# A second SiLU matmul by one level of Strassen's algorithm, with the weight parts of the first one's stage spread between its products

## The chip, the cores and the metric

The kernel runs on one core of one Trainium2 chip. The metric is device microseconds from the start of the program to its end, as the median of three runs. The core's engines run their own instruction streams: TensorE (PE) multiplies, ScalarE (ACT), VectorE (DVE) and GpSimd (POOL) work on tiles element by element, and SyncE (SP) issues the DMA transfers. They wait for one another at semaphores.

## The reference

Pooled attention, then two feed-forward layers on 4608 tokens of width 512; every array is fp32:

```python
def _moe2_ref(x, w_in, w_out):          # x: 4608 x 512
    h = x @ w_in                        # w_in: 512 x 2048
    g = h * (1.0 / (1.0 + np.exp(-h)))  # SiLU
    return (g @ w_out)                  # w_out: 2048 x 512

def reference(**kwargs):
    attn_out = _attn_ref(q, k, v)       # 8 x 8 x 576 x 64, keys and values pooled by 8
    x = ...                             # 4608 x 512
    x = _moe_ref(x, ...)                # SoLU and layer norm, 512 -> 1024 -> 512
    return _moe2_ref(x, ...)
```

The change touches `_moe2_ref` alone.

## The kernel before, in words

An fp32 value is kept as two parts of type fp32r, hi and lo: hi is a copy made by ACT (`AF.Copy`), lo is the difference, made by DVE or POOL (`sub`). One fp32 product is three matmuls: hi with hi, hi with lo, lo with hi.

The program has three stages. The first computes attention and the SoLU layer and puts `x` into DRAM (`x2d`); it also turns the weights of the last two matmuls into fp32 and keeps them in DRAM (`w2if`, `w2of`). The change leaves it alone but for the shape of `w2of`.

The second stage is the first SiLU matmul, already done by one level of Strassen's algorithm (in Winograd's form: seven products and fifteen additions for eight products). It has 12 steps `n`: half the columns of `w_in` (`half`) by six groups `g` of 768 tokens. A step has four pairs `i`, and `hidden2(n, i, hooks)` computes one: seven products of six matmuls of 128x384, each into a PSUM bank, and the additions that combine them. DVE makes `u2`, `u3`, `gt[0,0]` (c11), `gt[0,1]` (c12) and `gt[1,0]` (c21) out of PSUM (L654), ACT copies `m1` and `m5`, POOL adds two. PE may be eight products ahead, since there are eight banks. Between these operations the four `hooks` stand, in which the parts for later products are made:

- `tokens(n + 1)`: sums and differences of the next step's token blocks (T1 to T4 on POOL), their hi copies on ACT, their lo parts on DVE (`lo`, L517, 128x768). They are given out over the four pairs. Raw tokens come by `load_tokens`, 1.5 MB into `x2r`, which has one buffer.
- `quad(q)`: the weight parts of a quarter of `w_in`, six functions, from `w2r` (one buffer, `load_quad`, 1 MB). `quad(1)` is made ahead of the stage; `quad(2)` between the pairs (5,2), (5,3) and (6,0), and `quad(3)` after (6,0) and (6,1).
- in n=11, where no tokens are left, the hi and lo parts of the first seven blocks of `w_out` (`split_w2o`, lo on POOL).

When a pair is over, ACT applies SiLU and SP stores the 768 KB of `gt` to `gd` in DRAM (`finish_pair`, called in the next pair).

The third stage is the second SiLU matmul. `project2(c, f)` multiplies block `f` (of 16) of chunk `c` (of 9, 512 tokens each) by `w_out`: four PSUM banks, three matmuls of 128x512 each, 1728 matmuls in all (L722). Two steps ahead of it, `split_g` makes hi (ACT, L117) and lo (DVE, L118) of g, which `load_g` reads back from `gd` in loads of four blocks. The other nine blocks of `w_out` are split beside the first steps. `store2` copies the four banks (two by ACT, two by DVE) and stores 256 KB each.

PE follows program order throughout. From the second stage on ACT, DVE, POOL and SP follow it too (`manual_schedule`), so an instruction that waits holds up everything behind it on its engine.

Of the kernel before, what the change touches and what calls it, by code (L numbers as in the profile page):

```python
# [89 lines left out]
):  # L90
    nc = tc.nc
    const = ctx.enter_context(tc.tile_pool(name="const", bufs=1, side="left"))
    stage = ctx.enter_context(tc.tile_pool(name="stage", bufs=2, side="left"))
# [582 lines left out]
    w2oh, w2ol = {}, {}
    graw, g_t, o_t = {}, {}, {}

    w2s = {}

    def load_w2o(f):
        w2s[f] = stage.tile([P, DM], F32, tag="w", name="w2s", bufs=3)
        nc.sync.dma_start(w2s[f], w2of[f])

    def split_w2o(f):
        if f < 7:
            t = pools["te"].tile([P, 2, DM], F32R, tag=f"t{f}", name="w2o")
        else:
            t = pools["w2o"].tile([P, 2, DM], F32R, tag=f"w2o{f}", name="w2o")
        w2oh[f], w2ol[f] = t[:, 0], t[:, 1]  # L690
        nc.scalar.activation(w2oh[f], w2s[f], AF.Copy)
        sub(nc.gpsimd, w2ol[f], w2s[f], w2oh[f].bitcast(F32))

    def load_g(c, b):
        if (c, b) == (0, 0):
            raw = pools["x2r"].tile([P, 4, GO], F32, tag="x2r", name="gr")
        else:
            raw = pools["gr"].tile([P, 4, GO], F32, tag=f"gr{b % 3}", name="gr")
# [8 lines left out]
    def split_g(c, f):
        gh = pools["gs"].tile([P, GO], F32R, tag=f"gh{f % 4}", name="gh")
        gl = pools["gs"].tile([P, GO], F32R, tag=f"gl{f % 4}", name="gl")
        split(gh, gl, graw[c, f // 4][:, f % 4])  # L710
# [2 lines left out]
    def project2(c, f):
        gh, gl = g_t.pop((c, f))
        if f == 0:
            o_t[c] = [bank("op") for t in range(4)]
        for t in range(4):
            ts = slice(t * P, (t + 1) * P)
            for m, (l, r) in enumerate(
                ((gh[:, ts], w2oh[f]), (gh[:, ts], w2ol[f]), (gl[:, ts], w2oh[f]))  # L720
            ):
                nc.tensor.matmul(  # L722
                    o_t[c][t], l, r, start=(f == 0 and m == 0), stop=(f == FC2 - 1 and m == 2)
                )

    def store2(c):
        for t in range(4):
            ob = pools["out"].tile([P, DM], F32, tag=f"ob{t}", name="ob")
            if t % 2:
                nc.vector.tensor_copy(ob, o_t[c][t])  # L730
            else:
                nc.scalar.activation(ob, o_t[c][t], AF.Copy)
            r0 = c * GO + t * P
            nc.sync.dma_start(out[r0 : r0 + P], ob)
# [154 lines left out]
    load_tokens(1)
    for f in quad(1):  # L890
        f()
    N2 = NSUB * NG2
    for n in range(N2):
        work = tokens(n + 1) if n + 1 < N2 else [[] for _ in range(4)]
        if n == 0:
            work = [[], work[0], work[1], [lambda a=a, b=b: (a(), b()) for a, b in zip(work[2], work[3])]]
        for i in range(NPAIR):
            if (n, i) == (0, 0):
                continue
            if (n, i) in ((NG2 - 1, 0), (NG2, 0)):  # L900
                load_quad(2 + (n == NG2))
            hooks = work[i]
            if n == N2 - 1:
                for f in range(2 * i, min(2 * i + 2, 7)):
                    load_w2o(f)
                    hooks = hooks + [lambda f=f: split_w2o(f)]
            hidden2(n, i, hooks)
            if (n, i) in ((NG2 - 1, 2), (NG2, 0)):
                q2 = quad(2 + (n == NG2))
                for f in q2[:3]:  # L910
                    f()
# [10 lines left out]
    open_pool("gr", 1, "right")
    open_pool("w2o", 1, "right")
    open_pool("out", 1, "right")
    steps = [(c, f) for c in range(NGO) for f in range(FC2)]
    LAG = 2
    load_g(0, 1)
    for i in range(len(steps) + LAG):
        if i < len(steps):
            c, f = steps[i]  # L930
            if i < 9:
                load_w2o(i + 7)
            if f % 4 == 0 and i + 8 < len(steps):
                load_g(steps[i + 8][0], steps[i + 8][1] // 4)
            split_g(c, f)
            if i < 9:
                split_w2o(i + 7)
        if i >= LAG:
            c, f = steps[i - LAG]
            project2(c, f)  # L940
            if f == FC2 - 1:
                store2(c)


# [38 lines left out]
```

## Time and profile before

| | us |
|---|---|
| median of three runs (1421.16, 1422.57, 1426.73) | 1422.57 |
| the profiled execution | 1423.88 |
| its span in the trace | 1422.1 |
| PE busy (7416 matmuls) | 1321.4, 93% |
| DVE busy | 787.4, 55% |
| ACT busy | 647.5, 46% |
| POOL busy | 537.6, 38% |

The second stage lies at 614 to 1016 of the span, the third from there to the end. A busy share is a mean over stages that differ; which engine the end waits for is to be read stage by stage from the chain, from the idle times in front of PE's instructions, and from the timeline. Matmuls overlap, so what one costs is the distance from one to the next and not its own duration.

### The profile page before, as it was taken

The numbers are of one execution on the slowest core, as the hardware profiler recorded it, in microseconds if no ns is written. First come the engines' busy times: TensorE is split into PE (matmuls) and PEld (weight loads), VectorE is DVE, ScalarE is ACT, GpSimd is POOL, SyncE is SP. The second block draws the span as 40 slices with busy tenths as digits, with TensorE's granted clock in tenths as the row PEclk, the third lists the DMA queues.
The fourth block names the chain that finished last, engine by engine and source line by source line (L and its number), as shares of the span: only waits on it lengthen the run. The fifth ranks groups of instructions, "written<-read, shape, count | busy, mean of one in ns | idle before, by whom it ended". The sixth has DMA issues, their size and how long they took to land.

```text
span 1422.1 us, 20311 instructions
## 1 busy us (share of the span) xinstructions
PE 1321.4 (93%) x7416; PEld 1192.7 (84%) x7416; DVE 787.4 (55%) x1161; ACT 647.5 (46%) x1624; POOL 537.6 (38%) x737
## 2 busy tenths in 40 slices
PE   2689999999999998999899979999899999999998
PEld 2478789988989897998899969999788888888887
DVE  6896566757756556247677676766343222222222
ACT  4784656555555555344444544445432222222221
POOL 5674443535444335226556656656430000000000
PEclk9799999999999999999999999999899999999999
DMA  6655154534433201033434543444733444214440
GB/s 223 209 171 163 59 156 134 156 119 133 147 104 112 89 31 60 30 119 122 160 134 155 186 141 133 156 158 172 240 111 104 148 148 148 90 61 146 148 148 30
DMA packets 85651, 186.91 MB, mean 131 GB/s; under 512 B 6192, under 2 KB 27696, under 8 KB 83504
## 3 DMA queue, kind: packets, MB, share of 16 engines
q1 hardware_dynamic: 85552, 185.63, 39.0%
q8 instruction: 58, 0.95, 0.3%
q14 instruction: 41, 0.34, 0.1%
HBM read 120.59 MB, written 65.01 MB: 131 GB/s over the span
## 4 chain that ended last, share of the span: by engine, by line
PE 55%; DVE 6%; DMA 3%; ACT 3%; issue 3%; POOL 1%; SPq 0%; DVEq 0%; ACTq 0%; POOLq 0%
PE op L722 27%; PE m L644 15%; PE xp L498 6%; PE hp L428 5%; DVE t L517 2%; DMA x2r<-x2d 2%; DVE gt L654 1%; PE tp L478 1%; DVE u L654 1%; DVE wt L517 1%; PE sp L299 1%; ACT w2s L538 1%; ACT gt L626 1%; PE av L403 0%; DVE w2s L517 0%
## 5 line engine op out<-in xcount | busy, mean ns | idle before, releaser
L644 PE MATMUL m<-t,w2s 128*128 128x384 f32 x2016 | 362.8, 340 | 23.5 <-DVE gt L654 8.0
L644 PEld LDWEIGHTS m<-t,w2s 128*128 128x128 f32 x2016 | 355.7, 191 | 30.2 <-DVE gt L654 11.3
L722 PE MATMUL op<-w2o,gh 128*128 128x512 f32 x1152 | 357.2, 392 | 6.6 <-ACT gh L117 6.6
L722 PEld LDWEIGHTS op<-w2o,gh 128*128 128x128 f32 x1152 | 217.8, 189 | 52.5 <-ACT gh L117 7.4
L118 DVE TENSOR_TENSOR gl<-gr,gh 128x512 fp32r<-128x512 f32 x144 | 106.4, 751 | 263.4 <-ACT gh L117 263.4
L722 PE MATMUL op<-w2o,gl 128*128 128x512 f32 x576 | 225.4, 391 | 0.2 <-DVE gl L118 0.2
L117 ACT ACTIVATE gh<-gr 128x512 fp32r<-128x512 f32 x144 | 89.0, 629 | 258.8 <-PE op L722 208.3
L498 PE MATMUL xp<-lnh,w1oh 128*128 128x256 f32 x576 | 168.1, 292 | 0.6 <-ACT lnh L117 0.3
L498 PE MATMUL xp<-lnl,w1oh 128*128 128x256 f32 x576 | 164.3, 285 | 1.2 <-DVE lnl L118 1.2
L498 PE MATMUL xp<-lnh,w1ol 128*128 128x256 f32 x576 | 164.1, 285 | 0.0
L654 POOL TENSOR_TENSOR gt<-u,m 128x384 f32<-128x384 f32 x96 | 120.1, 1271 | 115.4 <-DVE u L654 76.6
L722 PEld LDWEIGHTS op<-w2o,gl 128*128 128x128 f32 x576 | 108.7, 189 | 23.7 <-DVE gl L118 1.1
L428 PE MATMUL hp<-w1ih,xTh 128*128 128x512 f32 x288 | 119.8, 416 | 7.9 <-DVE e L447 7.8
L428 PE MATMUL hp<-w1il,xTh 128*128 128x512 f32 x288 | 115.9, 402 | 0.6 <-POOL w1il L150 0.6
L428 PE MATMUL hp<-w1ih,xTl 128*128 128x512 f32 x288 | 115.9, 402 | 0.0
L317 ACT ACTIVATE pr<-sp,st 128x72 f32<-128x72 f32 x288 | 88.3, 331 | 59.0 <-POOL st L309 58.8
L498 PEld LDWEIGHTS xp<-lnl,w1oh 128*128 128x128 f32 x576 | 111.7, 194 | 1.5 <-DVE lnl L118 1.4
L498 PEld LDWEIGHTS xp<-lnh,w1oh 128*128 128x128 f32 x576 | 111.5, 194 | 1.7 <-DVE lnl L118 1.1
L498 PEld LDWEIGHTS xp<-lnh,w1ol 128*128 128x128 f32 x576 | 111.7, 194 | 0.0
L672 ACT ACTIVATE gt<-gt 128x768 f32<-128x768 f32 x48 | 40.7, 847 | 148.6 <-DVE gt L654 148.6
L517 DVE TENSOR_TENSOR t<-x2r,t 128x768 fp32r<-128x768 f32 x36 | 60.4, 1679 | 25.5 <-ACT t L582 25.5
L428 PEld LDWEIGHTS hp<-w1ih,xTh 128*128 128x128 f32 x288 | 56.3, 195 | 20.4 <-issue 7.6
(109 smaller groups left out, 2098.9 us busy)
## 6 DMA issues: line engine op xcount, KB each, us to landing
gd<-gt SPq DMA_DIRECT2D x48, 768.0 KB, 4.2
gr<-gd SPq DMA_DIRECT2D x24, 1024.0 KB, 6.8
x2r<-x2d SPq DMA_DIRECT2D x12, 1536.0 KB, 8.1
gr<-gd SPq DMA_DIRECT2D x24, 512.0 KB, 6.2
q<-qT SPq DMA_DIRECT2D x36, 256.0 KB, 3.1
raw<-kT SPq DMA_DIRECT2D x32, 288.0 KB, 3.4
x2d<-xo SPq DMA_DIRECT2D x18, 512.0 KB, 3.4
out<-ob SPq DMA_DIRECT2D x36, 256.0 KB, 3.0
```

The lines of the kernel that those rows point to most:

```text
L117: nc.scalar.activation(hi, src, AF.Copy)
L118: nc.vector.tensor_tensor(lo, src, hi.bitcast(F32), op=ALU.subtract)
L299: nc.tensor.matmul(sp[done : done + n, p // 2, (p % 2) * 2 * SP : (p % 2 + 1) * 2 * SP], q[:, p, done : done + n], kbd[b % 2][:, p, :], st ...
L317: behind["ACT"] = nc.scalar.activation(pr[:, g, h], sv[:, g, h], AF.Exp, scale=SCALE, bias=st[:, 0, g, h : h + 1], accum_out=st[:, 1, g, h ...
L428: nc.tensor.matmul(hp[:, f], l, r, start=(n == 1 and m == 0), stop=(n == KC and m == 2))
L478: nc.tensor.transpose(tp[:, k * P : (k + 1) * P], e[:, f, k * P : (k + 1) * P], ident)
L498: nc.tensor.matmul(xp[:, :GW], l, r, start=(k == 0 and m == 0), stop=(k == FC1 - 1 and m == 2))
L517: eng.tensor_tensor(dst, a, b, op=ALU.subtract)
L644: nc.tensor.matmul(to, wt[:, a, o : o + P], tk[:, b, k], start=(k == 0 and m == 0), stop=(k == 1 and m == 2),)
L654: eng.tensor_tensor(dst, a, b, op=ALU.add)
L672: nc.scalar.activation(gt[:, 0], gt[:, 0], AF.Silu)
L722: nc.tensor.matmul(o_t[c][t], l, r, start=(f == 0 and m == 0), stop=(f == FC2 - 1 and m == 2))
```

## The change

The third stage gets Strassen's form too. A chunk of 512 tokens is two halves of 256, an output block is 256 columns, and the 16 blocks of f are four sets (`NSET`) of two blocks each from the upper and lower half of `w_out`. A product is 12 matmuls of 128x256: seven a set, 252 products in all, 3024 matmuls. A bank holds a product summed over the four sets of a chunk, so seven banks are in use.

- `sums_g(q)` makes S1 and S2 of a set's g on POOL (two 128x512 operations). `prepare(n)` makes the parts of product `n`: a copy by ACT, a difference by DVE, and before S3A and after A12 one more DVE operation. They go into a ring of nine (`NRING`), and `prepare(n + 9)` stands behind product `n`.
- `w2o_unit(fs, ...)` makes the weight parts for one or two f in seven functions: seven ACT copies, seven DVE subtractions, four POOL subtractions. For f = 0, 1 it runs in pair (11,0), for f = 2 in (11,1); `sums_g(0)` and `prepare` 0 to 6 in (11,2) and (11,3). f = 3 is made between products 0 to 6, f = 4, 5 between 7 to 13, f = 6, 7 between 14 to 20.
- `combine(c, j)` stands behind each product of a chunk's last set: five DVE adds out of PSUM, two ACT copies and two POOL adds a chunk, and two stores of 512 KB.
- In the second stage `quad(1)` goes into the hooks of (0,1), the tokens of n=1 into (0,2) and (0,3); in n=5 the tokens of n=6 into the first two pairs and `quad(2)` into the last two; in n=6 `quad(3)` into the first two and the tokens into the last two. `spread` deals the functions out over a pair's four hooks. `load_quad` makes two loads, for quad 2 behind (1,0), for quad 3 behind (5,3); `load_tokens(1)` stands ahead of `load_quad(1)`.
- At the hand-over, the pools of the second stage are closed, and `load_g(1)`, `load_g(2)` and the late weights stand on SP behind the last pair's store.

```diff
+NSET = FC2 // 4
+NRING = 9
...
     def load_quad(q):
-        w2r[q] = pools["wr"].tile([P, 4, 512], F32, tag="w2r", name="w2r")
-        nc.sync.dma_start(w2r[q], w2if[q])
+        w2r[q] = [pools["wr"].tile([P, 2, 512], F32, tag=f"w2r{h}", name="w2r") for h in range(2)]
+        for h in range(2):
+            nc.sync.dma_start(w2r[q][h], w2if[q][:, 2 * h : 2 * h + 2])
...
+    def w2o_unit(fs, load, to, temps):
...
+        def tmp(k, a, b):
+            t[k] = temps(k).rearrange("p (f d) -> p f d", d=256)[:, :n]
+            sub(nc.gpsimd, t[k], a, b)
+        def put(j, src):
+            w = to(j)
+            nc.scalar.activation(w[:, :, 0], src, AF.Copy)
+            sub(nc.vector, w[:, :, 1], src, w[:, :, 0].bitcast(F32))
...
+        def first():
+            tmp(1, b12, b11)
+            tmp(2, b22, t[1])
+            put(0, b11)
...
+    def sums_g(q, temps):
...
+        nc.gpsimd.tensor_tensor(s1, a21, a22, op=ALU.add)
+        sub(nc.gpsimd, s2, s1, a11)
...
+    def prepare(n):
...
+        if j == S3A:
+            sub(nc.vector, a21, a11, a21)
...
+        nc.scalar.activation(ring[n][:, 0], src, AF.Copy)
+        sub(nc.vector, ring[n][:, 1], src, ring[n][:, 0].bitcast(F32))
+        if j == A12:
+            sub(nc.vector, a12, a12, s2)
...
+    def product2(n):
...
+        for i in range(2):
+            w = wo[2 * s + i, j]
+            for h in range(2):
+                ts = slice(h * P, (h + 1) * P)
+                for m, (l, r) in enumerate(((0, 0), (0, 1), (1, 0))):
+                    nc.tensor.matmul(
+                        op[:, 256 * h : 256 * h + 256], t[:, l, i, ts], w[:, r],
...
+    load_tokens(1)
     load_quad(1)
-    load_tokens(1)
-    for f in quad(1):
-        f()
...
         if n == 0:
-            work = [[], work[0], work[1], [lambda a=a, b=b: (a(), b()) for a, b in zip(work[2], work[3])]]
+            work = [[], quad(1), work[0] + work[1], work[2] + work[3]]
+        elif n == NG2 - 1:
+            q2 = quad(2)
+            work = [work[0] + work[1], work[2] + work[3], q2[:3], q2[3:]]
+        elif n == NG2:
+            q3 = quad(3)
+            work = [[lambda: None] + q3[:3], q3[3:], work[0] + work[1], work[2] + work[3]]
+        elif n == N2 - 1:
...
+            g0 = [lambda: sums_g(0, wt_tmp)] + [lambda m=m: prepare(m) for m in range(7)]
+            work = [u0, u1, g0[:4], g0[4:]]
...
+            hidden2(n, i, spread(work[i]))
+            if n == 1 and i == 0:
+                load_quad(2)
+            if (n, i) == (NG2 - 1, NPAIR - 1):
+                load_quad(3)
...
+    load_g(1)
+    load_g(2)
...
+    late = late_w2o([3])
+    sums_g(1, s_tmp)
+    nxt = late_w2o([4, 5])
+    prepare(7)
+    prepare(8)
+    for n in range(NM):
...
+        product2(n)
+        if s == NSET - 1:
+            combine(c, j)
+        if q <= 2:
+            late[j]()
+        m = n + NRING
+        if m < NM:
...
+            prepare(m)
```

What stands in a row on DVE in pair (5,0), before. `u`, `m` and `gt` are the pair's additions, `t` the lo parts of the next step's tokens:

```order
L654 TENSOR_TENSOR u_8415<-m,m_8413 128x384
L654 TENSOR_TENSOR u_8416<-m,u_8415 128x384
L517 TENSOR_TENSOR t_8444<-x2r,t_8444 128x768
L654 TENSOR_TENSOR gt<-m,m_8413 128x384
L517 TENSOR_TENSOR t_8456<-x2r,t_8456 128x768
L654 TENSOR_TENSOR gt<-m,gt 128x384
L654 TENSOR_TENSOR gt<-m,u_8416 128x384
```

and now, where `tt` are the differences that POOL makes:

```order
L662 TENSOR_TENSOR u_8413<-m,m_8411 128x384
L524 TENSOR_TENSOR t_8442<-x2r,t_8442 128x768
L662 TENSOR_TENSOR u_8414<-m,u_8413 128x384
L524 TENSOR_TENSOR t_8445<-x2r,t_8445 128x768
L662 TENSOR_TENSOR gt<-m,m_8411 128x384
L524 TENSOR_TENSOR t_8469<-tt,t_8469 128x768
L662 TENSOR_TENSOR gt<-m,gt 128x384
L524 TENSOR_TENSOR t_8472<-tt,t_8472 128x768
L662 TENSOR_TENSOR gt<-m,u_8414 128x384
```

Four lo parts stand in the pair where two stood, two of them on POOL's differences of the same pair.

On SP at the hand-over from the second stage to the third, before (`gd<-gt` are the stores of g, `gr` the loads of it, `w2s` the weights):

```order
L627 DMA gd_90<-gt 256x1x768
L683 DMA w2s<-w2of_101 128x512
L627 DMA gd_90<-gt 256x1x768
L703 DMA gr<-gd_85 128x4x512
L627 DMA gd_90<-gt 256x1x768
L703 DMA gr<-gd_85 128x4x512
L683 DMA w2s<-w2of_102 128x512
L703 DMA gr<-gd_85 128x4x512
```

and now:

```order
L1024 DMA w2s<-w2of_97 128x1024
L635 DMA gd_89<-gt 256x1x768
L635 DMA gd_90<-gt 256x1x768 x4
L734 DMA gr<-gd_85 128x2x512 x4
L1052 DMA w2s<-w2of_98 128x2x512
L1052 DMA w2s<-w2of_99 128x2x512
L1052 DMA w2s<-w2of_100 128x2x512
L734 DMA gr<-gd_85 128x2x512 x2
```

The loads of two sets of g and of the weights of f = 3, 4, 5 moved behind the last store; before, one load of g stood ahead of the last store, and the weights came one block at a time.

On DVE, early in the third stage, before (`gl` is the lo part of g, `ob` the output):

```order
L118 TENSOR_TENSOR gl<-gr,gh 128x512 x18
L730 COPY ob<-op 128x512 x2
L118 TENSOR_TENSOR gl<-gr,gh 128x512 x16
L730 COPY ob<-op 128x512 x2
L118 TENSOR_TENSOR gl<-gr,gh 128x512 x16
```

and now, about products 7 to 13 (`w2o` the weights' lo parts, `gt` those of g's parts, `s` a sum made by POOL):

```order
L524 TENSOR_TENSOR gt_10811<-s,gt_10811 128x512
L524 TENSOR_TENSOR w2o<-wt,w2o 128x2x256
L524 TENSOR_TENSOR gr<-gr 128x2x256
L524 TENSOR_TENSOR gt_10830<-gr,gt_10830 128x512
L524 TENSOR_TENSOR w2o<-wt,w2o 128x2x256
L524 TENSOR_TENSOR gt_10850<-gr,gt_10850 128x512
L524 TENSOR_TENSOR gr<-gr,s 128x2x256
L524 TENSOR_TENSOR w2o<-wt,w2o 128x2x256
L524 TENSOR_TENSOR gt_10873<-gr,gt_10873 128x512
```

Weight parts moved to DVE and alternate there with the parts of g.

## Rows read from the trace of the kernel before

**Rows 1.** The page: chain that ended last, by engine and line (shares of the span)

```profile
PE 55%; DVE 6%; DMA 3%; ACT 3%; issue 3%; POOL 1%; SPq 0%; DVEq 0%; ACTq 0%; POOLq 0%
PE op L722 27%; PE m L644 15%; PE xp L498 6%; PE hp L428 5%; DVE t L517 2%; DMA x2r<-x2d 2%; DVE gt L654 1%; PE tp L478 1%; DVE u L654 1%; DVE wt L517 1%; PE sp L299 1%; ACT w2s L538 1%; ACT gt L626 1%; PE av L403 0%; DVE w2s L517 0%
```

**Rows 2.** Chain in order of time: start, length (us), engine, what, count

```profile
624.87 14.41 PE xp L498 x120
...
669.74 9.24 DMA x2r<-x2d
...
684.76 55.33 PE m L644 x312
...
1027.91 390.33 PE op L722 x1714
```

**Rows 3.** Windows: stretch, length, then busy us (instructions) of PE, PEld, DVE, ACT, POOL

```profile
614.00:1015.50 401.50, 378.03 (x2147) 370.95 (x2145) 262.36 (x345) 190.33 (x306) 240.56 (x160) 0.97 0.42 153
639.10:685.10 46.00, 37.87 (x207) 36.21 (x206) 30.15 (x37) 20.16 (x33) 27.66 (x17) 0.94 0.32 115
795.00:833.60 38.60, 32.87 (x177) 31.69 (x176) 27.29 (x36) 19.28 (x32) 21.30 (x15) 0.96 0.50 185
833.60:870.10 36.50, 30.24 (x146) 29.10 (x146) 27.32 (x35) 17.97 (x30) 25.30 (x16) 0.86 0.37 124
990.20:1016.10 25.90, 25.32 (x147) 25.00 (x145) 10.95 (x21) 13.98 (x24) 16.76 (x15) 1.00 0.66 216
1031.50:1422.10 390.60, 386.73 (x1707) 319.86 (x1705) 114.49 (x159) 98.72 (x163) 10.65 (x7) 1.00 0.35 117
```

**Rows 4.** PE's waits in 614 to 1016: waited for, total us, times, longest

```profile
PE m L644 <- DVE gt L654: 8.0, 7, 5.2
...
PE m L644 <- ACT w2s L538: 6.2, 2, 3.2
```

**Rows 5.** Timeline, DVE around n=10: start, length, operation [idle before <- releaser]

```profile
959.97 0.54 DVE L654 TENSOR_TENSOR gt<-m,u 128x384 f32<-128x384 f32 x1
962.07 0.56 DVE L654 TENSOR_TENSOR u<-m,m 128x384 f32<-128x384 f32 x1 [1.56 <-ACT m L660]
...
989.66 0.54 DVE L654 TENSOR_TENSOR gt<-m,u 128x384 f32<-128x384 f32 x1
```

**Rows 6.** Timeline, POOL in the first pair of that stretch

```profile
962.86 1.99 POOL L654 TENSOR_TENSOR gt<-u,m 128x384 f32<-128x384 f32 x2 [2.87 <-DVE u L654]
964.80 1.85 POOL L517 TENSOR_TENSOR tt<-x2r 128x768 f32<-128x768 f32 x1
966.73 2.45 POOL L517 TENSOR_TENSOR tt<-x2r,tt 128x768 f32<-128x768 f32 x1
```

**Rows 7.** Timeline, DVE subtractions of 128x512 one behind another, quad 1

```profile
611.29 0.69 DVE L517 TENSOR_TENSOR w2s<-w2r,w2s 128x512 fp32r<-128x512 f32 x1
611.89 0.70 DVE L517 TENSOR_TENSOR wt<-w2r 128x512 f32<-128x512 f32 x1
```

**Rows 8.** Timeline, POOL and DVE early in the second SiLU matmul

```profile
1026.04 1.27 POOL L517 TENSOR_TENSOR w2o<-w2s,w2o 128x512 fp32r<-128x512 f32 x1 [10.71 <-ACT w2o L691]
1029.37 6.39 POOL L517 TENSOR_TENSOR w2o<-w2s,w2o 128x512 fp32r<-128x512 f32 x4 [2.06 <-DMA w2s<-w2of]
...
1029.85 6.46 DVE L118 TENSOR_TENSOR gl<-gr,gh 128x512 fp32r<-128x512 f32 x4 [1.99 <-ACT gh L117]
```

**Rows 9.** Timeline, SP, PE and ACT at the hand-over to the second matmul

```profile
1017.08 0.52 SPq L627 DMA_DIRECT2D gd<-gt  x1
...
1017.89 1.22 PE L722 MATMUL op<-w2o,gh 128*128 128x512 f32 x2 [2.37 <-ACT gh L117]
...
1025.34 0.63 ACT L691 ACTIVATE w2o<-w2s 128x512 fp32r<-128x512 f32 x1 [7.50 <-DMA w2s<-w2of]
```

**Rows 10.** The page, DMA issues: count, KB each, median us to landing

```profile
x2d<-xo SPq DMA_DIRECT2D x18, 512.0 KB, 3.4
out<-ob SPq DMA_DIRECT2D x36, 256.0 KB, 3.0
```

More of the change, by code (lines that the diff above doesn't have):

```diff
@@ L674, in hidden2, with third, sixth, load_g @@
         last.append((gt, g, half * NPAIR + i))
[L676 to L687, printed above, removed]
-        else:
[L689 to L698, printed above, removed]
+    wo, graw, ring = {}, {}, {}
+    def w2o_unit(fs, load, to, temps):
+        n = len(fs)
+        half = load()
+        b11, b12, b21, b22 = (half[i][:, :, 256 * j : 256 * j + 256] for i in range(2) for j in range(2))
+        t = {}
+        def tmp(k, a, b):
[5 more added lines that the diff above has]
+            sub(nc.vector, w[:, :, 1], src, w[:, :, 0].bitcast(F32))
+            for i, f in enumerate(fs):
+                wo[f, j] = w[:, i]
+        def first():
+            tmp(1, b12, b11)
+            tmp(2, b22, t[1])
+            put(0, b11)
+        def third():
+            tmp(3, b22, b12)
+            put(2, t[1])
+        def sixth():
+            tmp(4, b21, t[2])
+            put(5, b22)
+        return [
+            first, lambda: put(1, t[2]), third, lambda: put(3, t[3]),
+            lambda: put(4, b21), sixth, lambda: put(6, t[4]),
+        ]
+    def load_g(q):
+        c, s = divmod(q, NSET)
+        if q % 3 == 0:
+            raw = pools["x2r"].tile([P, 2, 2, GO], F32, tag="x2r", name="gr")
+        else:
+            raw = pools[f"gr{q % 3}"].tile([P, 2, 2, GO], F32, tag="gr", name="gr")
         done = 0
@@ L713, in project2 @@
[L713 to L734, printed above, removed]
+        graw[q] = raw
@@ new lines, in pooled_attention__solu__silu_kernel @@
+    o_t = {}
+    def product2(n):
+        q, j = divmod(n, 7)
+        c, s = divmod(q, NSET)
+        if s == 0:
+            o_t[c, j] = bank("op")
+        op = o_t[c, j]
+        t = ring.pop(n)
+        for i in range(2):
+            w = wo[2 * s + i, j]
+            for h in range(2):
+                ts = slice(h * P, (h + 1) * P)
+                for m, (l, r) in enumerate(((0, 0), (0, 1), (1, 0))):
+                    nc.tensor.matmul(
+                        op[:, 256 * h : 256 * h + 256], t[:, l, i, ts], w[:, r],
+                        start=(s == i == h == m == 0),
+                        stop=(s == NSET - 1 and i == h == 1 and m == 2),
+                    )
@@ new lines, in pooled_attention__solu__silu_kernel, with combine, temp, add @@
+    m_t = {}
+    def combine(c, j):
+        b = o_t.pop((c, j)).rearrange("p (h d) -> p h d", h=2)
+        def temp(name):
+            m_t[name] = pools["m2"].tile([P, 512], F32, tag=name, name=name).rearrange(
+                "p (h d) -> p h d", h=2)
+            return m_t[name]
+        def add(eng, dst, x, y):
+            eng.tensor_tensor(dst, x, y, op=ALU.add)
+        if j == 0:
+            m_t["o"] = pools[f"ob{c % 2}"].tile([P, 2, 2, DM], F32, tag="ob", name="ob")
+            nc.scalar.activation(temp("m1"), b, AF.Copy)
+            return
+        c11, c12, c21, c22 = (
+            m_t["o"][:, h, :, 256 * d : 256 * d + 256] for h in range(2) for d in range(2)
+        )
+        r0 = c * GO
+        rows = [out[r0 + 256 * h : r0 + 256 * h + 256].rearrange("(t p) d -> p t d", p=P) for h in range(2)]
+        if j == 1:
+            add(nc.vector, temp("u2"), b, m_t["m1"])
+        elif j == 2:
+            nc.scalar.activation(temp("m5"), b, AF.Copy)
+            add(nc.gpsimd, c12, m_t["u2"], m_t["m5"])
+        elif j == 3:
+            add(nc.vector, temp("u3"), b, m_t["u2"])
+            add(nc.gpsimd, c22, m_t["u3"], m_t["m5"])
+        elif j == 4:
+            add(nc.vector, c11, b, m_t["m1"])
+        elif j == 5:
+            add(nc.vector, c12, b, c12)
+            nc.sync.dma_start(rows[0], m_t["o"][:, 0])
+        else:
+            add(nc.vector, c21, b, m_t["u3"])
+            nc.sync.dma_start(rows[1], m_t["o"][:, 1])
@@ L899, in pooled_attention__solu__silu_kernel @@
                 continue
[L900 to L911, printed above, removed]
@@ L922, in pooled_attention__solu__silu_kernel @@
[L922 to L942, printed above, removed]
+    sg.close()
@@ new lines, in pooled_attention__solu__silu_kernel, with late_w2o, load, to @@
+    for name in ("gr1", "ob0", "gr2", "m2", "ob1", "w2o"):
+        open_pool(name, 1, "left")
+    load_g(1)
+    load_g(2)
+    def late_w2o(fs):
+        n = len(fs)
+        def load():
+            w = pools[f"ob{fs[0] // 2 % 2 ^ 1}"].tile([P, 2, 2, DM], F32, tag="ob", name="w2s")
+            for i, f in enumerate(fs):
+                nc.sync.dma_start(w[:, :, i], w2of[f])
+            return [w[:, h, :n] for h in range(2)]
+        def to(j):
+            return pools["w2o"].tile([P, n, 2, 256], F32R, tag=f"w{fs[0]}{j}", name="w2o")
+        tags = ["u2", "m1", "u3", "m5", "u2"]
+        return w2o_unit(fs, load, to, lambda k: pools["m2"].tile([P, 512], F32, tag=tags[k], name="wt"))
```

84 lines of the change are left out of this document (64 added, 20 removed).

## The prediction

> **What bounds the kernel now.** I read the page's chain first, to see which engine the end hangs on: TensorE (PE) holds 55% of the span, and the second SiLU matmul, L722, is the longest single item [rows 1]. The chain in order of time then gives prices: 1714 matmuls of 128x512 follow one another for 390.33 us, 0.2277 us each, with hardly an idle moment, while 120 matmuls of 128x256 with a new stationary block for each take 14.41 us, 0.1201 us each [rows 2]. So the last 400 us are bound by PE alone, and whatever lowers PE's work there shows in the time until another engine is late. At 1031.50 to 1422.10 VectorE (DVE) is busy 114 of 391 us and GpSimd (POOL) 11 [rows 3]: there is room.
>
> The first SiLU matmul is a different case. Its Strassen products go through DVE: a pair of seven products ends with the add that reads `u3` (c21), and the next pair's first add waits 1.56 us for a ScalarE (ACT) copy, not for PE [rows 5]. Four pairs lie between 959.97 and 989.66, 29.7 us; PE needs 28 x 6 matmuls at 55.33/312 = 0.177, 29.8 us. The two are level, and PSUM lets PE run up to eight products ahead of DVE. Anything that lengthens DVE's chain by more than that lead is paid. PE's waits in this stage, 8.0 us for DVE and 6.2 us for weight parts [rows 4], are all that a better spreading could remove there.
>
> **The change part by part.** The sum is made against the span of 1422.1 us (the profiled execution took 1423.88, the median is 1422.57: three numbers 0.1% apart).
>
> *Fewer matmul columns.* 1728 x 0.2277 = 393.5 us go; 9 chunks x 4 sets x 7 products x 12 = 3024 matmuls of 128x256 at 0.1201 come, 363.1 us. The size is the traced one, with its weight loads in it, so I take it whole: -30.4. (Half of a 128x512 matmul, 0.114, would save 18 us more; the measured row speaks against it.) A product lasts 12 x 0.120 = 1.44 us, a set of seven 10.1.
>
> *The products' start.* Call the end of the last c21 C (1016.1). Today the first matmul of L722 starts 1.8 us after C (1017.89), and the span ends 406 us after C [rows 3, 9], some 4 us of it a last copy and a store. After the change, g for sets 1 and 2 and the weights of f=3 are queued on SP behind the store of the last pair, which waits for that pair's SiLU. How long do they take? Today the store of 0.79 MB, a 1.05 MB load and a 0.26 MB weight land 8.26 us after 1017.08 [rows 9]. Of this some 2.6 us are fixed, since a copy of 512 KB takes 3.4 against 3.0 for 256 KB [rows 10]. The rate is then 2.1/5.7 = 0.37 MB/us, and store, two sets and the f=3 weights, 3.4 MB, land at C+1+9.2+2.6, about C+13. Sets 0 to 2 also carry the late weights: per set 7 ACT copies, 7 DVE and 4 POOL subtractions beside 7 `prepare` steps (9 DVE operations) and 2 POOL adds. DVE subtractions of 128x512 follow one another every 0.61 us alone, but when POOL reads two tiles at the same time four of them take 6.46 us and POOL's four 6.39, against 0.69 and 1.27 alone [rows 7, 8]. A meeting thus costs DVE at most 1.0; not every POOL operation has DVE beside it from end to end, and I take 0.85. So one set of the full kind costs DVE 16 x 0.61 = 9.8, six meetings 5.1, and 0.9 of waits for ACT (copies of 0.63 [rows 9]): 15.7, over PE's 10.1. The first set has half-size parts: 12. Product 27, the last that needs a new weight, ends at C + 13 + 12 + 2 x 15.7, about C+57, instead of C+40. The other 224 products take 322.8 us, and I allow 3 for waits at chunk ends: C+383. Against C+402 today: **-19.3**, the saving of matmuls included. Bounds: without any meeting 5 us less in each of two full sets, 10 better; with an ACT copy unhidden in each of 16 steps of them, 10 worse.
>
> *Steady products.* Per set DVE then has 9 x 0.61 = 5.5, two POOL adds met (1.1 to 1.8) and 1.5 of waits: 8.2 to 8.8. A chunk's last set adds 5 combining adds of some 0.7 (0.56 for 128x384 out of PSUM [rows 5], a third more columns) and two POOL adds: 12.7. The mean is 9.3 to 9.9 us against PE's 10.1, so this is hidden, by little. The new wait is that of the combining adds for their product: `prepare` of the product nine ahead stands behind it on DVE, and PE waits for that; nine ready products are 13 us of cover.
>
> *n=5 and n=6.* The subtractions for quads 2 and 3 leave the block between pairs, and the tokens are packed two pairs' worth into one. PE lost 5.7 and 6.3 us here today (38.6 and 36.5 long, 32.87 and 30.24 busy [rows 3]). But doubled tokens ask, inside one pair, for POOL's differences T1 and T2 (1.85 and 2.45 us, behind two adds [rows 6]), ACT's copy of them and DVE's subtraction. Walking (5,0): the wait for m1 1.6, u2 0.6, R11 with its wait for x2r and its copy 4.0, u3 0.6, then POOL's add and T1 3.0, T1's copy and subtraction 2.4, T2's in turn 2.4, c21 0.6: 15.2. The other seven pairs, walked likewise, give 8.3, 7.9, 9.3, 8.6, 9.3, 13.3 and 8.3: 80.2 against 75.1, and 1.7 for a later load for n=7. **+6.8**. From below, PE's 59.6 us and twelve weight operations hidden only partly give -11; with every POOL meeting paid, +14.
>
> *n=0.* Quad 1 moves from ahead of the stage into pair (0,1), where PE was already waiting. Tokens of n=1 end later, so x2r is free 3.9 us later for the next load, which today already shows on the chain as 9.24 us [rows 2]. **+3.9**; the stretch holds 46 us for 37.87 busy [rows 3], and this lies between -5 and +8.
>
> *n=11.* Today the shortest stretch, 25.9 us [rows 3], since there are no tokens left: 6.5 a pair. Now pair (11,0) takes 7 weight subtractions (4.3), two meetings (1.8) and 1.6 waiting for data: 14.2. (11,1), at half size, 8.5; (11,2) three `prepare` steps 7.8; (11,3) four 9.3. 39.8 in all: **+14.0**. If PE's lead covered all but its own 29.8, +3; with each POOL operation met, +18. What is bought here is the start above: without early weights it would be later still.
>
> *Tail.* The last store has 512 KB in place of 256: +0.4 [rows 10].
>
> On SP, `load_tokens(1)` now stands ahead of `load_quad(1)`, and the load of quad 2 moves to (1,0), where its buffer has long been read: both cost nothing. The load of quad 3 leaves only when POOL's last subtraction of quad 2 in (5,3) has read the buffer; the next tokens' load and g's stores queue behind it. It lands inside (6,0), where I count 2 us for it, and the 1.7 above is the tokens' part.
>
> Sum: -19.3 + 6.8 + 3.9 + 14.0 + 0.4 = **+5.8**: a saving of 30 us of matmuls that the work around them eats. 1422.6 + 5.8 = 1428.
>
> *A rule to weigh.* Rows show DVE and POOL each lasting 1.6 us when they meet, four by four [rows 8]. The Trainium skill, "SBUF — State Buffer", section "SBUF: two separate sides", calls the shared port pair an exclusive lock: whoever starts first has it for the whole instruction, the other fully blocks. By that a meeting lasts both durations together.
>
> **The rivals.** *R1, the spreading hides.* The first stage's added stretches fit in PE's lead, POOL's differences come in time, and n=5, 6, 0 and 11 cost nothing: 5.8 - 24.7, some **1404**. For it: DVE is busy 262 of 401 us there [rows 3], so the work itself has room. Against: the chain of rows 5 is of waits, not of work, and each doubled pair adds links to it.
> *R2, slower: DVE sets the pace of the second stage for good.* It decides when DVE's mean set exceeds 10.1 us; my sum is 9.3 to 9.9. With one more meeting per set (0.85) and a wait for ACT it is 10.8, and 33 sets x 0.7 = 23 more: **1451**. For it: 1.6 us meetings [rows 8]; against: 9 products ready.
> *R3, meetings by lock.* 0.69 + 1.27 = 1.95 us instead of 1.61, 0.34 on each of about 18 meetings of the first three sets, 6 us: **1434**. It decides if meetings with POOL cost DVE the whole of POOL's operation. The rows contradict the amount, so it has little. The rule named above would give this time; the trace's four-by-four times disagree with it by 0.34 each.
>
> **How the numbers follow.** My sum (1418 to 1438): 0.50. R1 0.25, R2 0.17, R3 0.08. The likeliest is my sum: 1428. The range leaves out R1's lower half (0.1) and R2's upper (0.1): 1403 to 1448. A measurement of this kernel tells 0.5%, 7 us: faster lies below 1415.5, slower above 1429.7. Faster: R1 and a little of mine, 0.27. Slower: R2, R3 mostly, and 0.18 of mine: 0.40. Same 0.33.
>
> **What would show it.** In the trace of after: 128x256 matmuls spaced 0.120 us in the last 320 us with PE over 97% busy there (right), or PE waits for DVE's `gt` inside steady chunks (R2). From the last c21 to the product 27: 57 us, with PE waits for w2o or DVE (right), 41 (wrong, R1). c21 to c21: 80 for n=5 and 6, 40 for n=11; if these read 65 and 29, R1. DVE and POOL operations of 1.6 us when together, 1.95 for R3. If the 128x256 spacing comes out near 0.114, or waits on the chain are for loads that I took as landed, the sum is wrong.

## The result and the profile after

The changed kernel takes 1437.2 us (median of four runs, 1433.8 to 1438.2) against 1423.7 for the kernel before (four runs): a ratio of 1.0090, 95% interval 1.0063 to 1.0117. It is slower by 0.9%, inside the range and 9 us above the forecast of 1428. The profiled execution of after is the fastest of its four (1433.8, span 1432.0); against the span of 1422.1 before, the two traces differ by 9.9 us.

First the page's chain by engine and by line, then PE's waits from the last pair on (waited for: us in total, times, longest), after:

```profile
PE 44%; DVE 10%; issue 5%; DMA 4%; ACT 4%; POOL 3%; SPq 0%; DVEq 0%; ACTq 0%; POOLq 0%
PE op L782 22%; PE m L652 9%; PE xp L505 6%; PE hp L435 5%; DVE t L524 3%; DMA x2r<-x2d 3%; DVE gt L662 2%; DVE gt L524 1%; DVE u L662 1%; DVE w2o L524 1%; PE tp L485 1%; POOL tt L524 1%; DVE wt L524 1%; ACT t L590 1%; DMA w2s<-w2of 1%
```

```profile
PE op L782 <- DVE w2o L524: 10.2, 13, 1.7
PE op L782 <- ACT w2o L699: 7.1, 4, 4.7
PE op L782 <- ACT gt L763: 6.3, 1, 6.3
```

Against [rows 1], PE's share of the chain fell from 55 to 44% and DVE's rose from 6 to 10%. These 23.6 us of waits for weights (`w2o`) and for g's parts (`gt`) all lie in the first 60 us behind the last pair.

The stages as windows of after (stretch, length, then busy us and instructions of PE, PEld, DVE, ACT, POOL, then the granted clock), to be read against [rows 3]:

```profile
797.10:878.30 81.20, 68.46 (x353) 62.37 (x352) 53.07 (x71) 37.78 (x61) 45.33 (x30) 0.96 0.36 131
996.90:1041.30 44.40, 38.80 (x221) 36.22 (x220) 27.68 (x44) 20.69 (x38) 20.70 (x18) 0.92 0.34 126
1041.30:1055.60 14.30, 3.37 (x18) 2.65 (x17) 1.39 (x3) 2.51 (x5) 2.89 (x3) 0.66 0.88 307
1055.60:1101.20 45.60, 32.85 (x222) 29.15 (x223) 42.33 (x46) 22.23 (x44) 25.55 (x18) 0.96 0.28 94
1101.20:1427.60 326.40, 326.06 (x2714) 325.51 (x2712) 259.83 (x333) 134.07 (x239) 119.22 (x80) 1.00 0.38 123
```

They are n=5 and 6, n=11, the time from the last c21 (C) until DVE has the first weight of f=3, from there to the end of product 27, and the other 224 products. From c21 to c21 in both traces:

| stretch | before | after | difference | forecast |
|---|---|---|---|---|
| to the end of n=1 | 704.8 | 706.8 | +2.0 | +3.9 |
| n=5 and 6 | 75.0 | 81.1 | +6.1 | +6.8 |
| n=2 to 4 and 7 to 10 | 210.5 | 209.0 | -1.4 | 0 |
| n=11 | 25.9 | 44.4 | +18.5 | +14.0 |
| C to the end | 406.0 | 390.7 | -15.3 | -18.9 |
| sum | 1422.1 | 1432.0 | +9.9 | +5.8 |

(Rounded one by one. Of the first row's 2.0 us, 1.4 lie ahead of the stage's first c21, at 624.0 before and 625.4 after.)

The products themselves are as forecast. In the chain in order of time (start, length, what, count) one load and the long run of matmuls read:

```profile
1045.77 9.34 DMA w2s<-w2of
...
1113.42 314.16 PE op L782 x2616
```

314.16/2616 is 0.1201 us a matmul, the figure of [rows 2]; PE is busy 326.06 of 326.40 us behind product 27.

### The profile page after: what moved, and what is told of

It is laid out like the page before. It is cut to its first block, busy times and chain, and to the rows that moved or that the text cites. A ratio compares the mean times of both kernels' runs of the same rounds, so it can differ in the third digit from the quotient of the medians.

```text
span 1432.0 us, 23554 instructions
## 1 busy us (share of the span) xinstructions
PE 1308.0 (91%) x8712; PEld 1236.4 (86%) x8712; DVE 988.0 (69%) x1403; ACT 710.4 (50%) x1751; POOL 672.3 (47%) x831
## 4 chain that ended last, share of the span: by engine, by line
PE 44%; DVE 10%; issue 5%; DMA 4%; ACT 4%; POOL 3%; SPq 0%; DVEq 0%; ACTq 0%; POOLq 0%
PE op L782 22%; PE m L652 9%; PE xp L505 6%; PE hp L435 5%; DVE t L524 3%; DMA x2r<-x2d 3%; DVE gt L662 2%; DVE gt L524 1%; DVE u L662 1%; DVE w2o L524 1%; PE tp L485 1%; POOL tt L524 1%; DVE wt L524 1%; ACT t L590 1%; DMA w2s<-w2of 1%
## 5 line engine op out<-in xcount | busy, mean ns | idle before, releaser
L652 PE MATMUL m<-t,w2s 128*128 128x384 f32 x2016 | 371.3, 343 | 30.6 <-DVE gt L662 27.3
L782 PE MATMUL op<-w2o,gt 128*128 128x256 f32 x3024 | 371.4, 285 | 24.0 <-DVE w2o L524 10.2
L782 PEld LDWEIGHTS op<-w2o,gt 128*128 128x128 f32 x3024 | 366.3, 193 | 29.1 <-DVE w2o L524 13.3
L524 DVE TENSOR_TENSOR gt<-gr,gt 128x512 fp32r<-128x512 f32 x180 | 173.6, 996 | 59.3 <-ACT gt L763 59.3
L763 ACT ACTIVATE gt<-gr 128x512 fp32r<-128x512 f32 x180 | 103.9, 623 | 153.6 <-DVE gr L524 132.7
L744 POOL TENSOR_TENSOR s<-gr 128x512 f32<-128x512 f32 x35 | 56.7, 1620 | 112.4 <-DMA gr<-gd 62.7
L662 DVE TENSOR_TENSOR u<-m,m 128x384 f32<-128x384 f32 x48 | 26.8, 558 | 85.0 <-ACT m L668 70.0
L524 DVE TENSOR_TENSOR t<-tt,t 128x768 fp32r<-128x768 f32 x48 | 74.5, 1553 | 11.2 <-ACT t L590 11.0
```

The lines of the kernel that those rows point to most:

```text
L652: nc.tensor.matmul(to, wt[:, a, o : o + P], tk[:, b, k], start=(k == 0 and m == 0), stop=(k == 1 and m == 2),)
L662: eng.tensor_tensor(dst, a, b, op=ALU.add)
L744: nc.gpsimd.tensor_tensor(s1, a21, a22, op=ALU.add)
L763: nc.scalar.activation(ring[n][:, 0], src, AF.Copy)
L782: nc.tensor.matmul(op[:, 256 * h : 256 * h + 256], t[:, l, i, ts], w[:, r], start=(s == i == h == m == 0), stop=(s == NSET - 1 and i == h ...
```

## The experiments

The theory was that DVE's chain is what the end waits for, from n=0 until product 27, and PE behind it. The rivals were that the added stretches are covered by PE's lead (R1), or that DVE paces the steady products as well (R2). The kernels were compared with the kernel before on the chip that they ran on (1421.4 us in the first group, 1422.9 in the second).

**The first stage's places undone.** `quad(1)`, the doubled tokens and `quad(2)`, `quad(3)` go back to where they stood; the rest as changed.

```diff
+    load_quad(1)
     load_tokens(1)
-    load_quad(1)
+    for f in quad(1):
+        f()
...
-            work = [work[0] + work[1], work[2] + work[3], q2[:3], q2[3:]]
...
+            if (n, i) in ((NG2 - 1, 2), (NG2, 0)):
+                q2 = quad(2 + (n == NG2))
...
```

> The changed kernel with the weight parts and tokens of the first SiLU stage (n=0, 5, 6) put back where they stood; n=11 and the Strassen second matmul as changed. Theory (each doubled pair adds links to the chain POOL, ACT, DVE, and this chain is the path): the changed trace ends n=1 2.0 us later than before and takes 81.1 us for n=5 and 6 against 74.9, so putting them back gives 8.2 us: about 1429 us median, 1.004 of before. Rival (these stretches are covered by PE's lead or by waits that come later anyway): no change, 1437.

Measured: 1424.8 us, ratio 1.0021 (0.9999 to 1.0042), 9.8 us (0.0069 of 1421) below the changed kernel's ratio. n=5 and 6, in its trace (columns as above), are back at 75 us:

```profile
791.20:866.20 75.00, 63.66 (x329) 60.91 (x328) 55.60 (x71) 37.08 (x61) 46.55 (x30) 0.91 0.43 156
986.10:1030.80 44.70, 39.15 (x222) 36.31 (x220) 27.66 (x44) 20.66 (x38) 20.84 (x18) 0.92 0.34 124
```

The theory holds and R1 falls for these three steps. n=11 is as long as in the changed kernel: 44.6 us from c21 to c21.

**The same places alone.** The kernel before with only the spreading of n=0, 5 and 6.

```diff
+            work = [[], quad(1), work[0] + work[1], work[2] + work[3]]
+        elif n == NG2 - 1:
+            q2 = quad(2)
+            work = [work[0] + work[1], work[2] + work[3], q2[:3], q2[3:]]
+        elif n == NG2:
+            q3 = quad(3)
+            work = [[lambda: None] + q3[:3], q3[3:], work[0] + work[1], work[2] + work[3]]
...
```

> The kernel before with only the new places of the weight parts and tokens in n=0, 5 and 6; second matmul and n=11 as before. Theory (the two parts of the change add up): the changed trace lost 2.0 us by the end of n=1 and 6.2 in n=5 and 6, and putting them back gave 9 us; alone they cost 8 to 10, ratio 1.006 to 1.007. Rival (the places only cost in company with the work that the Strassen form adds in n=11 and behind it): no change, 1.000.

Measured: 1433.9 us, ratio 1.0080 (1.0056 to 1.0103), 11 us. The parts add up: 1.0080 alone and 1.0021 for the rest, against 1.0090 together. Of the change's cost the spreading has nearly all; the Strassen form with its start is about even.

Why it costs shows in pair (5,0) of the changed kernel, DVE first and then POOL (start, length, operation, idle before and who ended it):

```profile
796.60 0.54 DVE L662 TENSOR_TENSOR gt<-m,u 128x384 f32<-128x384 f32 x1
...
802.01 0.96 DVE L524 TENSOR_TENSOR t<-x2r,t 128x768 fp32r<-128x768 f32 x1 [2.75 <-ACT t L590]
...
807.88 1.79 DVE L524 TENSOR_TENSOR t<-tt,t 128x768 fp32r<-128x768 f32 x1 [3.11 <-ACT t L590]
...
812.09 0.54 DVE L662 TENSOR_TENSOR gt<-m,u 128x384 f32<-128x384 f32 x1
```

```profile
805.13 1.84 POOL L524 TENSOR_TENSOR tt<-x2r 128x768 f32<-128x768 f32 x1
807.05 1.81 POOL L524 TENSOR_TENSOR tt<-x2r,tt 128x768 f32<-128x768 f32 x1
```

DVE stands 2.75 us for the raw tokens' copy, and 3.11 us for the copy of T1, which POOL had only finished at 807.0. From c21 to c21 it is 15.5 us, where before it was 10.4; 15.2 were forecast.

**The early parts behind the last pair.** What ran in the hooks of n=11 runs behind it. The loads stay in n=11; the pools are reordered so that later loads need not wait for the buffers that are read, and `load_g(2)` moves behind the load of f=3.

```diff
-            work = [u0, u1, g0[:4], g0[4:]]
+            behind_c = u0 + u1 + g0
...
     finish_pair()
+    for f in behind_c:
+        f()
     bt.close()
     sg.close()
-    for name in ("gr1", "ob0", "gr2", "m2", "ob1", "w2o"):
+    for name in ("ob1", "gr2", "m2", "gr1", "ob0", "w2o"):
...
```

> The early weight parts (f = 0, 1, 2) and the parts of products 0 to 6 are taken out of the hooks of n=11 and run behind the last pair, their loads staying where they are; pools reordered so that the loads of g set 1 and of f=3 need not wait for the buffers that these parts read. Theory: n=11 falls from 44.4 back to 26 to 30 us, and the moved work fills the 14 us after the last c21 in which DVE did two operations, ending some 18 to 21 us after it instead of the loads' 14.3: net 9 to 15 us less, about 1425. Rival (the work lies on the path wherever it stands): 1437, within 3.

Measured: 1428.1 us, ratio 1.0049 (1.0031 to 1.0067), 5.8 us below the changed kernel: between the two expectations. In its trace the last c21 and the first late weight part (f=3) on DVE:

```profile
1018.37 0.56 DVE L662 TENSOR_TENSOR gt<-m,u 128x384 f32<-128x384 f32 x1 [0.42 <-PE m L652]
...
1044.00 0.42 DVE L524 TENSOR_TENSOR w2o<-w2s,w2o 128x256 fp32r<-128x256 f32 x1
```

PE's longest wait there (columns as above):

```profile
PE op L782 <- ACT gt L763: 12.2, 1, 12.2
```

n=11 is back at 25.9 us, as expected. But the moved work lasts 25 us on DVE, not 18 to 21, so late parts begin 25.1 us behind C where they had begun 14.3 behind it: 18.5 us gained, 10.8 given back. What I had left out are more meetings with POOL, whose operations now follow one another beside DVE's: between C and the first late part DVE has 25 operations, which alone, at 0.60 for 128x512 and 0.34 for 128x256, would take some 13 us by my estimate. The run with three edits, further down, bears this out: without POOL's differences DVE has 37 operations there and needs 2 us less.

**Differences by DVE.** The four differences of each weight unit, and S1 and S2 of sets 0 to 3, move from POOL to DVE.

```diff
-            sub(nc.gpsimd, t[k], a, b)
+            sub(nc.vector, t[k], a, b)
...
-        nc.gpsimd.tensor_tensor(s1, a21, a22, op=ALU.add)
-        sub(nc.gpsimd, s2, s1, a11)
+        eng = nc.vector if q <= 3 else nc.gpsimd
+        eng.tensor_tensor(s1, a21, a22, op=ALU.add)
+        sub(eng, s2, s1, a11)
```

> The differences for the weight parts, and S1 and S2 of sets 0 to 3, are made by DVE instead of POOL. Theory (a meeting costs each engine about 1 us, so six POOL operations a set cost DVE more than doing them itself): a late set, 17.15 us in the changed trace, falls to 22 x 0.61 + 0.9 = 14.3, 2.5 such sets give 7; n=11 loses its waits for POOL and gains operations, 0 to -3. In all 1428 to 1431. Rival (DVE is the late engine, and six more operations a set make it later): 15 more DVE operations of 0.61 and up, 1444 to 1448.

Measured: 1426.9 us, ratio 1.0039 (1.0024 to 1.0054), 7.2 us less than the changed kernel, as the theory had it. DVE got more operations and was sooner done. First the changed kernel, where a set lies from one `gr<-gr` to the next, and POOL beside it:

```profile
1073.43 1.77 DVE L524 TENSOR_TENSOR gr<-gr 128x512 f32<-128x512 f32 x1
...
1080.83 1.75 DVE L524 TENSOR_TENSOR w2o<-w2s,w2o 128x512 fp32r<-128x512 f32 x1
1082.50 1.78 DVE L524 TENSOR_TENSOR gt<-gr,gt 128x512 fp32r<-128x512 f32 x1
1084.20 1.74 DVE L524 TENSOR_TENSOR w2o<-w2s,w2o 128x512 fp32r<-128x512 f32 x1
...
1090.58 1.78 DVE L524 TENSOR_TENSOR gr<-gr 128x512 f32<-128x512 f32 x1
```

```profile
1081.99 1.74 POOL L524 TENSOR_TENSOR wt<-w2s 128x512 f32<-128x512 f32 x1
1083.81 1.59 POOL L524 TENSOR_TENSOR wt<-w2s,wt 128x512 f32<-128x512 f32 x1
```

Then the experiment:

```profile
1066.99 0.68 DVE L524 TENSOR_TENSOR gr<-gr 128x512 f32<-128x512 f32 x1
...
1075.33 0.68 DVE L524 TENSOR_TENSOR wt<-w2s,wt 128x512 f32<-128x512 f32 x1
1075.93 0.68 DVE L524 TENSOR_TENSOR w2o<-w2s,w2o 128x512 fp32r<-128x512 f32 x1
...
1081.46 1.78 DVE L524 TENSOR_TENSOR gr<-gr 128x512 f32<-128x512 f32 x1
```

A set took 17.15 us (1073.43 to 1090.58) and takes 14.47. With POOL beside it a DVE subtraction starts 1.67 to 1.70 us behind the one before, alone 0.60. The last row shows the remaining meeting, with a sum that POOL still makes: 1.78. n=11 gains less, 42.0 us against 44.4: without POOL's differences its first pair still takes 15.4, with 3.6 us of DVE's waits for the loads of the weights and eleven operations in that one pair.

**More work for DVE in the steady stretch.** From set 5 on, each product's lo part is made twice.

```diff
-        sub(nc.vector, ring[n][:, 1], src, ring[n][:, 0].bitcast(F32))
+        for _ in range(2 if q > NSET else 1):
+            sub(nc.vector, ring[n][:, 1], src, ring[n][:, 0].bitcast(F32))
```

> From set 5 on each product's lo part is made twice, one more DVE subtraction of 128x512 per product. Theory (in the steady stretch PE is the limit, with DVE 79% busy, about 8.0 us of PE's 10.1 a set): 7 more operations make DVE's set 12.3 to 13, so DVE takes the pace and 31 sets grow by 2.2 to 2.9 each: 1505 to 1527. Rival (nine products in the ring cover it, or DVE is late already): 1437 to 1445 in the first case, 7 x 0.61 x 31 = 132 more, 1569, in the second.

Measured: 1574.7 us, ratio 1.1084 (1.1050 to 1.1118), 141 us above the changed kernel's ratio, some 4.5 us a set: near the figure that I had given for "DVE is late already", and nearly double the theory's. The same window of both kernels, changed first:

```profile
1300.00:1420.00 120.00, 120.00 (x1003) 120.00 (x1002) 93.60 (x120) 49.26 (x87) 41.97 (x28) 1.00 0.35 115
```

```profile
1300.00:1420.00 120.00, 96.51 (x688) 90.56 (x688) 106.42 (x143) 35.14 (x64) 29.34 (x21) 0.91 0.27 88
```

In the changed kernel PE is busy every microsecond, so DVE was not late. The error was to take DVE's busy time, 93.60 of 120 us or 7.9 of a set's 10.1, for its pace. Its pace contains waits that more work doesn't fill: its own operation on `gr`, then ACT's copy, then its subtraction (0.78 us idle each time), and meetings with POOL. How near to PE's 10.1 that pace is, the next run tells.

**One more operation a set.** This tells how level they were: the same, for one product of seven.

```diff
+        for _ in range(2 if q > NSET and j == A22 else 1):
...
```

> The changed kernel with one more DVE subtraction of 128x512 per set, from set 5 on. Seven more per set cost 4.5 us a set, which puts DVE's own pace at 10.1 + 4.5 - 7 x 0.67 = 9.9 us a set. Theory (that pace): one more gives 10.5 against PE's 10.1, 31 sets x 0.4 = 12 us more than the changed kernel, ratio 1.015 to 1.019. Rival (a pace of 9.3, the lower end of the forecast): 9.95, still hidden, 0 to 2 us more, ratio 1.009 to 1.010.

Measured: 1450.3 us, ratio 1.0192 (1.0166 to 1.0217), 14.5 us above the changed kernel, 0.47 a set (0.3 to 0.6 by the two intervals). PE's waits in its steady stretch, none of more than 0.3 us in the changed kernel, now show (columns as above):

```profile
PE op L783 <- ACT gt L763: 10.4, 7, 1.7
PE op L783 <- DVE gt L524: 0.5, 1, 0.5
```

DVE's own pace can be read from the changed kernel's trace. Behind product 27 DVE still catches up, and PE has no wait there. (Later the four sets of a chunk take 40.3 us, PE's pace.) From `gr<-gr` to `gr<-gr` they are here

```profile
1154.72 0.68 DVE L524 TENSOR_TENSOR gr<-gr 128x512 f32<-128x512 f32 x1
1156.18 1.29 DVE L524 TENSOR_TENSOR gt<-gr,gt 128x512 fp32r<-128x512 f32 x2 [0.78 <-ACT gt L763]
...
1164.44 0.68 DVE L524 TENSOR_TENSOR gr<-gr 128x512 f32<-128x512 f32 x1
...
1172.49 0.68 DVE L524 TENSOR_TENSOR gr<-gr 128x512 f32<-128x512 f32 x1
...
1181.13 0.68 DVE L524 TENSOR_TENSOR gr<-gr 128x512 f32<-128x512 f32 x1
...
1193.37 0.68 DVE L524 TENSOR_TENSOR gr<-gr 128x512 f32<-128x512 f32 x1
```

That is 9.7, 8.1, 8.6 and, where a chunk is combined, 12.2 us: a mean of 9.66 with waits and meetings, against PE's 10.1. DVE's pace was hidden by 0.4 us a set. (The expectation's 9.9 was too high: in the run with seven operations a set took 14.6 us in the trace, 0.70 more for each, not 0.67.) The one operation then cost more than its 0.61: a chunk's four sets took 42.57 us in this run, 10.64 a set. Once a chunk DVE now stands 1.85 us, 0.15 at that place in the changed kernel, for ACT's copy of a sum; POOL made that sum late, since it had waited for a load of g. DVE, and then POOL:

```profile
1198.69 0.68 DVE L524 TENSOR_TENSOR gr<-gr 128x512 f32<-128x512 f32 x1
...
1208.52 1.29 DVE L524 TENSOR_TENSOR gt<-s,gt 128x512 fp32r<-128x512 f32 x2 [1.85 <-ACT gt L763]
...
1241.26 0.68 DVE L524 TENSOR_TENSOR gr<-gr 128x512 f32<-128x512 f32 x1
```

```profile
1204.42 1.70 POOL L744 TENSOR_TENSOR s<-gr 128x512 f32<-128x512 f32 x1 [9.20 <-DMA gr<-gd]
```

**Three edits together.** First stage as before, early parts behind the last pair, differences by DVE.

```diff
+    for f in quad(1):
+        f()
...
+            behind_c = u0 + u1 + g0
...
+            sub(nc.vector, t[k], a, b)
...
```

> The three edits together: first stage's places as before, early parts behind the last pair, differences for the weights and S1, S2 of sets 0 to 3 by DVE. Theory (DVE's time from the last pair on is the path, each edit shortens it): alone they gave 9.2, 5.9 and 7.3 us against the changed kernel's 1.009. Behind the last pair the early work took 25 us on DVE with POOL beside it; alone it is 33 operations, 21 us. Sum 22 to 26 us less: ratio 0.991 to 0.994. Rival (the third edit's gain was mostly n=11's waits for POOL, which the second removes too, so the gains overlap): 17 to 19 less, ratio 0.996 to 0.997.

Measured: 1411.5 us, ratio 0.9919 (0.9897 to 0.9941), 24 us below the changed kernel and 11 below the kernel before. The gains add up (9.8, 5.8 and 7.2 make 22.8). Late parts begin 23.1 us behind C, against 25.1 with the early parts moved alone.

**Part of the weights back in n=11.** As the last, but f = 0, 1 in the last three pairs of n=11.

```diff
-            behind_c = u0 + u1 + g0
+            work = [[], u0[:3], u0[3:5], u0[5:]]
+            behind_c = u1 + g0
```

> As the three edits together, but the weight parts of f = 0 and 1 (11 DVE operations, 6.7 us) go back into n=11, into its last three pairs. Theory (with nothing in the hooks, the pairs of n=11 are paced by PE at 7 us while DVE's own chain is some 4.3, so about 2.2 us of DVE work a pair are free when they wait for no other engine than ACT): 3 to 6 us less than the three edits. Rival (every operation in a hook is on the path, as it was in the changed kernel, where n=11 grew by 18.5 us): the same as the three edits, within 2.

Measured: 1404.9 us, ratio 0.9869 (0.9847 to 0.9891): 7 us below the three edits, a little more than expected, and 1.3% faster than the kernel before. n=11 lies between the first two rows, and the third is the first late part:

```profile
990.20 0.54 DVE L662 TENSOR_TENSOR gt<-m,u 128x384 f32<-128x384 f32 x1
...
1017.34 0.55 DVE L662 TENSOR_TENSOR gt<-m,u 128x384 f32<-128x384 f32 x1
...
1034.01 0.42 DVE L524 TENSOR_TENSOR wt<-w2s 128x256 f32<-128x256 f32 x1
```

n=11 grew by 1.2 us, from 25.9 to 27.1, for 11 operations on DVE; in the changed kernel 23 had cost 18.5. Late parts begin 16 us behind C, where they began 23 behind it with the three edits. The same eleven operations in the first pair of n=11, as in the run with the differences by DVE, made that pair 11 us longer (15.4 against 4.4 before). So they are nearly free when they are dealt out over pairs that PE paces, with their loads landed and no wait for POOL; which of these conditions does most was not tested one by one.

## Why the prediction was right, and where it was not

*Fewer columns*, -30.4: right. 3024 matmuls at 0.1201, the row of another line [rows 2] with the same shape.

*n=5 and 6*, +6.8: right, +6.1, and pair by pair (15.5, 7.8, 8.6, 9.3, 8.8, 9.5, 13.8, 7.8 us against 15.2, 8.3, 7.9, 9.3, 8.6, 9.3, 13.3, 8.3). The mechanism is shown by undoing it and by doing it alone. R1 falls: POOL's differences do come too late when tokens are doubled.

*n=0*, +3.9: the mechanism happened, the sum was smaller. n=0 takes 5.1 us more, but 4.5 of that return in n=1 against this trace of before. In the three experiments with the old places n=0 and 1 take 78.4 to 78.5 us together (80.2 in the trace of before), in those with the new ones 80.7 to 82.7 (80.8 in the trace of after): anything from 0.5 to 4 us, so the size of this term stays open.

*n=11*, +14.0: mis-sized, +18.5, just past the far bound of +18. Its first pair took 15.9 us and not 14.2, the second 10.0 and not 8.5, the third 9.1 and not 7.8. (Before, the four took 4.4, 6.9, 7.3 and 7.3, so the 6.5 a pair of the forecast was a mean, and the first pair grew by 11.5.) The rows of the first pair, POOL and then DVE:

```profile
1001.94 1.30 POOL L524 TENSOR_TENSOR wt<-w2s 128x512 f32<-128x512 f32 x1 [1.65 <-DMA w2s<-w2of]
1003.48 1.45 POOL L524 TENSOR_TENSOR wt<-w2s,wt 128x512 f32<-128x512 f32 x1 [0.24 <-DMA w2s<-w2of]
```

```profile
1002.56 1.23 DVE L524 TENSOR_TENSOR w2o<-w2s,w2o 128x512 fp32r<-128x512 f32 x1 [3.50 <-ACT w2o L699]
...
1005.63 2.48 DVE L524 TENSOR_TENSOR w2o<-wt,w2o 128x512 fp32r<-128x512 f32 x2 [1.38 <-ACT w2o L699]
```

DVE waits 3.50 us for the first weight, where I had 1.6 for data: its load was late, for ACT's copy of it began only at 1001.89. It waits a further 1.38 for ACT, which copies a difference of POOL's, and for such a copy again 2.41 us in the second pair and 2.75 in the third. I had counted meetings, but not the chain POOL, ACT, DVE inside a weight unit and behind a sum of g's parts, although the same chain was in my walk of (5,0).

*The start*, C+57: the last of PE's waits for a weight ends at 1099.78, in front of product 27, which so ended at C+59.9:

```profile
1099.78 10.46 PE L782 MATMUL op<-w2o,gt 128*128 128x256 f32 x85 [1.68 <-DVE w2o L524]
```

The loads landed at C+13.8 (1055.1) instead of C+13, and a full set took 17.15 instead of 15.7, since a meeting was 1.7 us, not the 1.61 of [rows 8], and more operations met. That is 2.9 of the 3.6 us that this term missed. That meetings make the difference is shown by the run without them.

On the lock of R3: alone, the two operations take 0.60 from start to start (DVE) and last 1.27 (POOL) [rows 7, 8], 1.87 together; where they alternate, either engine starts its next one 1.67 to 1.82 behind the last. The Trainium skill, "SBUF — State Buffer", section "SBUF: two separate sides", has the loser block fully; the trace comes within 0.05 to 0.2 us of that, nearer than [rows 8] did, so R3's mechanism had more in it than I gave it. That its 1434 lies close to the measured time is luck all the same: a meeting cost DVE some 0.1 us more than the 1.61 of the sum, about 2 us on 18 meetings, not 6.

*Steady products*, hidden "by little": right, in the size too. DVE's mean set was 9.66 us, where 9.3 to 9.9 were forecast, 12.2 where 12.7 was put on a chunk's last set. R2 did not happen, and would have with one more operation a set. The step that held was to count waits and meetings into DVE's pace; the expectation for the run with seven operations forgot them and fell short by nearly half.

*The sum*: +5.8 forecast, +9.9 in the traces, +13.5 between the medians. That the sum came within some 4 us of the traces is luck in part: n=11 and the start were 8.1 us too low together, n=0, n=5 and 6 and the untouched steps 4.0 too high. Between trace and medians 3.6 us are not explained: the profiled execution was the shortest of four, and no trace shows which stretch differs in the others. Five traces whose kernels agree up to there have the first c21 of the second stage anywhere from 621.0 to 625.4, so some of the scatter lies ahead of all that the sum is about. The sign came out as the largest of my three chances, slower, though the predicted time itself lay at the edge of "same".

## What to carry to other kernels

Saving an eighth of the multiplications of a stage that PE bounds is worth what the makers of its operands can keep up with: add up the late engine's pace with its waits and meetings, not its busy time, before and behind the stage. In a stretch that DVE bounds, an operation given to POOL may be no relief if it meets DVE: here six fewer POOL operations and six more on DVE made a set 2.7 us shorter. And a piece of work put between products was nearly free here where PE paced them and the work waited neither for POOL nor for a load: walk one such pair by hand, from c21 to c21, before packing two into one.

## What the runs showed of the hardware that was not expected

A DVE subtraction of 128x512 fp32 and a POOL operation on two tiles, each in a row, fell into step at 1.67 to 1.82 us from start to start: DVE loses a factor of nearly three (0.60 alone), POOL a third (1.27 alone).

In the 14 us behind C PE did almost nothing. Its granted clock read 1.00 (2.4 GHz) up to 1044, 0.50 (1.2 GHz) from 1046 to 1058, and 1.00 again from 1060; 24 matmuls from 1055.66 on took 5.02 us, where they take 2.9 at the full clock. Nothing of this shows in the time: PE waited for DVE's and ACT's weight parts right behind them.
